# Two attention blocks on one core: when x's columns, q's pieces and small softmax steps are asked for in the v stage, and a new table of the main loop's order

## The chip, the cores and the metric

The kernel runs on one core of a Trainium2 chip. A core has five engines that each run their own instructions in program order: TensorE (PE in the profile, its weight loads PEld), VectorE (DVE), ScalarE (ACT), GpSimd (POOL) and SyncE (SP), which here starts nearly all transfers. The metric is the device time of one execution in microseconds; lower is better.

## The reference

Two independent attention blocks of 32 heads with 20 elements per head are computed on x of 2048 rows and 640 columns, and their outputs stand side by side. Block A looks at 8 earlier rows at a distance of 2 (a window); block B looks at all 2048 rows.

```python
# A
qkv = (x @ wqkv).reshape(B, S, 3, H, Dh)
idx = pos[:, None] - (jnp.arange(8) * 2)[None, :]
logits = einsum("bhsd,bhswd->bhsw", q, k[idx]) * Dh ** -0.5    # masked where idx < 0
a = einsum("bhsw,bhswd->bhsd", softmax(logits), v[idx]) @ wo
# B
scores = einsum("bhqd,bhkd->bhqk", q, k) * Dh ** -0.5
b = einsum("bhqk,bhkd->bhqd", softmax(scores), v) @ wo
return concatenate([a, b], axis=-1)
```

## The kernel before

All matrix products in fp32 are made of three products of a rounded high part and the rest (the list `PASSES`): high x high, high x rest, rest x high. A source that comes from memory lands in a staging tile `stg`; ScalarE copies it to the high part, and VectorE or GpSimd subtracts the high part from it for the rest. The stages, in order:

1. q and k of A, then q and k of B, for all rows. B's results go out to memory (`qb_d`, `kb_d`) and come back as stacks `bq` and `bk` of four heads (`b_pieces`). A stack of q has 16 pieces, four for each quarter of the rows.
2. **The v stage.** v of A and of B is computed in 15 blocks. Block 2c + half takes the column set c of x (0 to 3 are A's, 4 to 7 B's; a set is 512 rows of x, transposed, tiles `xn` and `xl`) and one half of the v weights (tiles `ww`). Each block has four ticks. In blocks 0 and 1 a tick is one group of 15 matmuls; from block 2 on a tick is 30 matmuls on half the array each, followed by four matmuls of one step of B's row maxima (`b_max`), which VectorE reduces (tile `mx`, two instructions a tick). `v_tick` closes a tick: it runs what is due then (`after(n, ...)` puts a step off by n ticks), asks for pieces of q, and lets GpSimd's work on A go on (`a_pace`, with an account of GpSimd's time, `gp.us`).
3. **The main loop**, 512 steps for B's 8 groups of heads. Each step needs four tiles of exponentials (tile `e`, ScalarE), four of maxima (VectorE), and four matmuls with v. The order of the tiles of 488 steps stands in a string, `ORDER`: S is two tiles for exponentials, M and N two tiles for maxima (reduced in one instruction or in two), Y one of each, V the step's matmuls with v, H a piece of A's output product, j a transpose for it; the digits are PSUM banks. The last 24 steps and B's last output follow from a plain loop.

GpSimd works through A's windows all this time: for each of 16 row tiles four units of scores (`akv` times `aq`, four adds, `al`) and four of values (`akv` times `al`, two adds), and the softmax between them; the reduce and the reciprocal of that softmax are VectorE's (`soft_jobs`). It also adds up B's parts (`braw`, `more`) and makes the rests of x's sets and of the v weights.

What the steps below touch: `x_load(c, w)` takes a set's tiles, asks for its three staging tiles at once and puts their copies and subtractions off by w ticks; it is called for set 1 after the first tick of block 0, and for set c + 2 at the end of block 2c + 1, each time with its copies one block later. `w_load(half, w)` does the same for B's v weights: half 0 at the end of block 4, nine ticks off; half 1 in the middle of block 7, four ticks off. Their subtractions, and those of sets 1 to 7, are GpSimd's. All transfers named here go through SP's queue in program order.

Of the kernel before, what the change touches and what calls it, by code (L numbers as in the profile page):

```python
# [75 lines left out]
def attention_pair(ctx, tc, xa, wqk_a, wv_a, wo_a, xb, wqk_b, wv_b, wo_b, oa, ob):  # L76
# [21 lines left out]
    soft_jobs, turn_jobs = [], []  # L98

# [478 lines left out]

    groups = 0
    gp.us = 0.0  # L580
    for m in range(0, 10, 2):
        nxt = []
        for n in range(4):
            for j in range(2):
# [355 lines left out]
    for block in range(15):  # L940
        c, half = divmod(block, 2)
        s0 = c % 4 * 4
        if block < 2:
            for s in range(s0, s0 + 4):
                v_group(c, half, s)
                v_tick(2.2, False)
                if (block, s) == (0, 0):
                    x_load(1, 5)
        else:
            ps4 = [bank() for _ in range(4)]  # L950
            for second in range(2):
                for u in range(2):
# [45 lines left out]
    def begin(i):  # L998
# [29 lines left out]
        "Y07M1S36Y54V0Y71S26M4Y03V7Y06M4S31Y72V0Y13M4S76VY71M2S64S05N17V6Y04M2S51VY70M4S13S26N07V1Y25S04N36VY07S25M3Y61"  # L1028
        "V0Y72M3S56VY75M1Y63S04V5Y06M1S74VY07S64M1Y35V0Y74S16Y23VM4S73Y61V2jY70M4S31VY07Y63M4S12S70Y63jV1jS72jM4Y03VM6"
        "S52Y40V3Y71jM5S24VY70M1S46S35Y07V4S31jM6Y52VY03S71Y65jM3S02Y57V1jM3S06Y72VjM3S05Y26V7Y01M3jS56VY05M1S36Y47V5"  # L1030
        "Y03M1S64VY07S64S31N25Y70V6jM4S32M0VS75M3S26jY01jV7jY25M3S61VY02S65M3jS71V0Y26M3S75VY71Y26H54Y30H54S71H54Y62H54"
        "Y73H54M1Y06V3Y74M1S05VY07M4S61Y23V7Y60S15N42VN06S51H43Y27H43Y05H43Y61Y27H43H43M5Y01V2Y73S04M5VY70M3Y15S62V0Y17"
        "M3S62VY71M5S24Y30V1Y27M5S43VY07H23N46S15H23Y70H23Y14H23Y56H23M0Y74V5S63M0Y72VS63Y74N01V2Y36S05Y74VM0S36Y54V7"
        "Y03M1S64VN06S53H42Y71H42Y05H42Y36Y71H42Y05H42Y36V7Y02M4S63VS06M2Y14V7M5S03Y21VM3S05Y62V1Y07M3S25VY07M5S42H31"
        "H31Y07H31Y24Y56H31Y07H31M4S26V0Y71S23M4VY71M2S46Y50V1Y74S26N35VY07S62M3H51H51Y07H51Y62M3H51Y07H51N62V0S17M3S56"
        "VM1S75Y43V6Y70S51M2VY70S15M2Y46V0S71jM2Y54VS71jY26S35N40V7jN64S21Y03VM5S42Y10V3jY47M5jS02VY70M1S64S53N07V6Y52"
        "S01M3VY70M1S53S46N07V5Y41M2S06VY70Y61S42Y35S07Y61N45V2Y01M3S75VY07S16M3S52N07V1S63M4Y02VY73S04M5Y21V7Y03M5S42V"
        "Y04M2S15Y76V0S15M2Y74VS15Y76Y23V0Y14S56N73VY71Y24H56Y03H56S71H56N42S03H56H56N74S01V2Y37M5S04VY70S13M5Y42V0Y17"
        "S63N54VY71M5S23Y40V1Y72S36N54VY07M5S23Y41V7Y02S63N54VN06S51H23Y74H23Y05H23Y16Y74H23Y05H23Y16V7Y02M4S63VY06S13"
        "M4Y27V6S01jM4S32jVjM0S75Y43V2jY01M6S35jVS01M3S57N62V0S13S45M6VM1S34Y76V5Y03S21N46VY70M2S14S65N07V1Y26S03M4VY07"  # L1040
        "M2S64S51N70V6Y52M3S71VY70M1Y53S46Y07V5Y64M1S03VY07M3S62S51Y07V6Y52S43N71VY70M4S32Y16V0Y73M4S21VY73M1S64H50H50"
# [145 lines left out]
```

## Time and profile before

| | us |
|---|---|
| median of three runs (1746.45 to 1746.90) | 1746.89 |
| the profiled execution | 1745.1 |
| its span from first to last instruction | 1742.9 |
| v stage with its blocks 2 to 14 and their tail, from 298.9 to 454.3 in the trace | 155.4 |
| main loop in the order of the table, 454.3 to 1626.0 | 1171.7 |

A row of the timeline is: start, length, engine, line, operation, output and input tiles, shape, count of instructions merged, and in brackets the idle time before it with what ended it. All instructions carry line 71, a helper that records them, so rows are told apart by the names of their tiles. A row of the windows gives each engine's busy time in a stretch, then the granted clock of TensorE, the busy share of the transfer engines, and GB/s.

### The profile page before, as it was taken

The page shows a single profiled execution, that of the slowest core. Times are in us where ns is not written, and L with a number is a line of the kernel's source. Part 1 is how long each engine was busy: PE and PEld are TensorE (multiplying, and loading weights), DVE is VectorE, ACT ScalarE, POOL GpSimd, SP SyncE. Part 2 cuts the span into 40 slices and gives each one's busy share as a digit, 9 for nine tenths or more (in the row PEclk, how much of TensorE's full clock was granted, in tenths as well). Part 3 has the DMA queues.
Part 4 walks back from the last instruction along what each step waited for, and adds up shares of the span by engine and source line. Part 5 has one row for each costly group of instructions (what it writes and reads, how often), then busy time and mean ns, then how long its engine had stood idle before and what let it go on. Part 6 is the DMA issues. An engine that isn't in the chain of part 4 may idle for free.

```text
span 1742.9 us, 34666 instructions
## 1 busy us (share of the span) xinstructions
PE 1726.1 (99%) x12711; PEld 1011.2 (58%) x12711; DVE 1349.3 (77%) x1818; ACT 1337.3 (77%) x2658; POOL 1271.9 (73%) x1125
## 2 busy tenths in 40 slices
PE   9999999999999999999999999999999999999999
PEld 8988888989635544444444443444444445444568
DVE  3113232888899999999999999999999999999300
ACT  4323223232599999999999999999999999999981
POOL 0000950999899999999999999999999953545242
PEclk9999999999999999999999999999999999999999
DMA  6447878657754263445435433543642532111123
GB/s 226 120 139 242 304 258 261 219 183 219 207 152 133 91 175 119 130 127 148 128 121 158 141 126 106 176 136 110 168 137 96 142 90 55 43 36 52 34 75 113
DMA packets 194435, 248.29 MB, mean 142 GB/s; under 512 B 89308, under 2 KB 114396, under 8 KB 193272
## 3 DMA queue, kind: packets, MB, share of 16 engines
q1 hardware_dynamic: 193688, 245.41, 46.6%
q8 instruction: 100, 1.64, 0.4%
q14 instruction: 71, 0.58, 0.1%
q10 hardware_dynamic: 576, 0.66, 0.1%
HBM read 181.08 MB, written 64.91 MB: 141 GB/s over the span
## 4 chain that ended last, share of the span: by engine, by line
PE 73%; POOL 17%; DMA 4%; issue 3%; DVE 2%; ACT 1%; SPq 1%; POOLq 0%; ACTq 0%; DVEq 0%
PE ps_st L71 73%; POOL akv L71 9%; POOL braw L71 4%; DVE mx L71 2%; POOL ao L71 1%; DMA stg<-xa 1%; SPq L71 1%; DMA mdr<-mtr 1%; DMA bq<-qb_d 1%; POOL ww L71 1%; POOL al L71 1%; ACT e L71 1%; DMA s_d<-braw 1%; POOL xn L71 0%; DMA s_d<-sm 0%
## 5 line engine op out<-in xcount | busy, mean ns | idle before, releaser
L71 DVE TENSOR_REDUCE mx<-ps_st 128x1 f32<-128x512 f32 (+1 forms) x1500 | 1227.5, 877 | 72.5 <-PE ps_st L71 61.4
L71 ACT ACTIVATE e<-ps_st 128x512 f32<-128x512 f32 x2048 | 1067.3, 630 | 32.5 <-PE ps_st L71 19.6
L71 PE MATMUL ps_st<-bk,bq 60*128 60x512 f32 x2048 | 555.1, 436 | 0.5 <-DVE mx L71 0.4
L71 PE MATMUL ps_st<-bq,bk 62*128 62x512 f32 x2048 | 548.7, 431 | 3.5 <-ACT e L71 1.8
L71 PE MATMUL ps_st<-e,vb 128*32 128x512 f32 x4096 | 543.1, 604 | 0.5
L71 PEld LDWEIGHTS ps_st<-bq,bk 62*128 62x128 f32 x2048 | 276.6, 184 | 401.6 <-ACT e L71 250.2
L71 POOL TENSOR_TENSOR braw<-braw,more 128x512 f32<-128x512 f32 x224 | 288.3, 1287 | 85.6 <-ACT more L71 85.1
L71 PEld LDWEIGHTS ps_st<-bk,bq 60*128 60x128 f32 x2048 | 257.9, 184 | 102.9 <-DVE mx L71 45.1
L71 POOL TENSOR_TENSOR akv<-akv,aq 128x1280 f32<-128x1280 f32 x64 | 188.4, 2944 | 166.4 <-DMA akv<-ka_d 166.3
L71 POOL TENSOR_TENSOR akv<-akv 128x640 f32<-128x640 f32 (+3 forms) x304 | 282.6, 930 | 14.7
L71 ACT COPY ro<-ps_st 128x320 f32<-128x320 f32 (+2 forms) x172 | 73.9, 465 | 185.9 <-PE ps_st L71 104.0
L71 PE MATMUL ps_st<-ww,xn 64*128 64x320 f32 (+1 forms) x1776 | 188.1, 311 | 6.5 <-POOL xn L71 2.4
L71 PEld LDWEIGHTS ps_st<-ww,xn 64*128 64x128 f32 (+1 forms) x1776 | 175.6, 187 | 22.6 <-ACT e L71 8.3
L71 PEld LDWEIGHTS ps_st<-e,vb 128*32 128x32 f32 x4096 | 82.2, 108 | 149.9 <-issue 77.1
L71 POOL TENSOR_TENSOR akv<-akv,al 128x1280 f32<-128x1280 f32 x64 | 151.6, 2368 | 0.1
L71 ACT COPY more<-ps_st 128x512 f32<-128x512 f32 x224 | 136.7, 610 | 4.0 <-POOL braw L71 2.0
L71 PE MATMUL ps_st<-xn,w 128*128 128x512 f32 x480 | 115.8, 390 | 0.0
L71 PEld LDWEIGHTS ps_st<-xn,w 128*128 128x128 f32 x480 | 90.1, 188 | 19.4
L71 POOL TENSOR_TENSOR xn<-stg,xn 128x512 fp32r<-128x512 f32 (+1 forms) x30 | 53.8, 1804 | 62.8 <-ACT xn L71 61.5
L71 PE MATMUL ps_st<-ww,aot 64*128 64x320 f32 x960 | 99.2, 308 | 0.0
L71 ACT CAST pr<-ps_st 128x512 fp32r<-128x512 f32 x40 | 23.5, 587 | 98.7 <-PE ps_st L71 93.0
L71 PEld LDWEIGHTS ps_st<-ww,aot 64*128 64x128 f32 x960 | 91.0, 186 | 4.6 <-DVE mx L71 0.5
(65 smaller groups left out, 1042.3 us busy)
## 6 DMA issues: line engine op xcount, KB each, us to landing
akv<-ka_d SPq DMA_DIRECT2D x128, 320.0 KB
akv<-va_d SPq DMA_DIRECT2D x128, 320.0 KB
kb_d<-pr SPq DMA_DIRECT2D x20, 512.0 KB
qb_d<-pr SPq DMA_DIRECT2D x20, 512.0 KB
bk<-kb_d SPq DMA_DIRECT2D x16, 640.0 KB
bq<-qb_d SPq DMA_DIRECT2D x64, 160.0 KB
stg<-xb SPq DMA_DIRECT2D x16, 512.0 KB
rb<-s_d SPq DMA_DIRECT2D x128, 64.0 KB
```

What stands on the lines that cost most here:

```text
L71: return self.tc.keep_in_program_order(op(*a, **k))
```

## The change

`x_load` is split. `x_raw(c)` takes only the three staging tiles and asks for them; `x_parts(c, raws)` later takes the set's tiles and issues copies and subtractions at once, with nothing put off. Set 1 is asked for in the last group but one of B's q and k, its parts come after the last tick of block 0, and their subtractions move from GpSimd to VectorE; set 2 is asked for at the same place. Set c + 2 is asked for after the first tick of block 2c + 1, and its parts come at that block's end. q's remaining 12 pieces are asked for one in a tick, and only in ticks with maxima (block 2 on), not two in each tick from block 0. VectorE's softmax steps in the v stage wait until they are due, where they had run at once. Half 0 of B's v weights is put off by eight ticks instead of nine. The string `ORDER` is new throughout; it has as many steps and as many pairs of tiles as before (Y, S, M and N: 698, 627, 444 and 127 before, 722, 615, 449 and 110 now, 1896 each time).

```diff
+    at_once = [True]
...
     def job(jobs, n, fn, *args):
         jobs.append((now[0] + n, fn, args))
-        if loop[0] is None:
+        if at_once[0]:
             run_jobs(jobs, 1)
...
+    def x_raw(c):
+        out = []
+        for a, b in PAIRS:
+            t = sb.tile([128, 1024], F32, tag="p", bufs=PB, name="stg")
+            raw = t[:, :(b - a) * 512].rearrange("p (k c) -> p k c", c=512)
+            sp.dma_start(raw, (xa, xb)[c // 4][a * 128:b * 128, c % 4 * 512:c % 4 * 512 + 512].rearrange("(k p) c -> p k c", p=128))
+            out.append((a, b, raw))
+        return out
...
                     elif g8 == 6:
                         for _ in range(4):
                             q_loads.pop(0)()
+                        xraw = x_raw(1)
...
     v_us = [40 * QK_US]
+    at_once[0] = False
...
-        for _ in range(min(2, len(q_loads))):
+        if maxima and q_loads:
             q_loads.pop(0)()
+        if soft_jobs and soft_jobs[0][0] <= now[0]:
+            run_jobs(soft_jobs, 1)
...
-    def x_load(c, w):
-        x, pieces = x_pieces((xa, xb)[c // 4], c % 4, gp)
-        XV.append((x, pieces))
-        wait[0] = w
-        for fn in pieces:
-            fn()
+    def x_parts(c, raws, second=gp):
+        t = columns(c % 4)
+        XV.append((t, None))
+        for a, b, raw in raws:
+            u, m = t[a // (KC - 1)], a % (KC - 1)
+            hi, lo = (u[:, x, m:m + b - a] for x in range(2))
+            act.copy(hi, raw)
+            second.tensor_tensor(lo, raw, hi.bitcast(F32), ALU.subtract)
...
-                if (block, s) == (0, 0):
-                    x_load(1, 5)
+                if (block, s) == (0, 3):
+                    x_parts(1, xraw, dve)
+                    xraw = x_raw(2)
...
                     v_tick(V_US)
+                    if half and c < 6 and not second and not u:
+                        xraw = x_raw(c + 2)
...
         if block == 4:
-            w_load(0, 9)
+            w_load(0, 8)
         if half:
             if c < 6:
-                x_load(c + 2, 4)
+                x_parts(c + 2, xraw)
...
     ORDER = (
-        "Y07M1S36Y54V0Y71S26M4Y03V7Y06M4S31Y72V0Y13M4S76VY71M2S64S05N17V6Y04M2S51VY70M4S13S26N07V1Y25S04N36VY07S25M3Y61"
+        "Y07S61M2Y45V0Y71S26M3Y05V7Y06M3S52Y71V0Y26M3S75VY71M5S24S03N17V2Y06S15Y34VM0S74Y56V3Y70S21N46VY70M4S12S63N07V1"
```

First place, SP at the change from B's q and k to the v stage, before (`pr` is a result of B's q, `ro` one of v's, `stg<-xa` a piece of set 1):

```order
L71 DMA bq_2015<-qb_d_70 20x1024
L71 DMA bq_2015<-qb_d_70 40x1024
L71 DMA qb_d_70<-pr_2153 128x2x512
L71 DMA va_d_69<-ro_2176 128x320
L71 DMA bq_2015<-qb_d_70 20x1024
L71 DMA bq_2015<-qb_d_70 40x1024
L71 DMA stg_2183<-xa 128x2x512
L71 DMA stg_2185<-xa 128x2x512
L71 DMA stg_2187<-xa 128x512
L71 DMA va_d_69<-ro_2204 128x320
```

The same place now:

```order
L71 DMA bq_2015<-qb_d_70 20x1024
L71 DMA bq_2015<-qb_d_70 40x1024
L71 DMA stg_2138<-xa 128x2x512
L71 DMA stg_2140<-xa 128x2x512
L71 DMA stg_2142<-xa 128x512
L71 DMA qb_d_70<-pr_2159 128x2x512
L71 DMA va_d_69<-ro_2182 128x320
L71 DMA va_d_69<-ro_2200 128x320
L71 DMA va_d_69<-ro_2224 128x320
L71 DMA va_d_69<-ro_2242 128x320
```

Set 1 moved ahead of a q store, a v store and two q pieces, and no q piece stands between the v stores any more.

Second place, GpSimd around half 1 of B's v weights, which block 9 needs, before (`ww_3323` is that half's rest, `xn_3415` and `xl_3416` that of set 5):

```order
L71 TENSOR_TENSOR akv_3099<-akv_3099,aq_2953 128x1280
L71 TENSOR_TENSOR ww_3323<-stg_3324,ww_3322 128x640
L71 TENSOR_TENSOR ww_3323<-stg_3326,ww_3322 128x640
L71 TENSOR_TENSOR ww_3323<-stg_3328,ww_3322 128x320
L71 TENSOR_TENSOR xn_3415<-stg_3417,xn_3415 128x1024
L71 TENSOR_TENSOR xn_3415<-stg_3419,xn_3415 128x1024
L71 TENSOR_TENSOR xl_3416<-stg_3421,xl_3416 128x512
L71 TENSOR_TENSOR akv_3099<-akv_3099 128x2x320
```

The same place now (`ww_3330` is the weights' rest, `xn_3431` and `xl_3432` set 5's):

```order
L71 TENSOR_TENSOR akv_3012<-akv_3012,aq_2872 128x1280
L71 TENSOR_TENSOR xn_3431<-stg_3286,xn_3431 128x1024
L71 TENSOR_TENSOR xn_3431<-stg_3288,xn_3431 128x1024
L71 TENSOR_TENSOR xl_3432<-stg_3290,xl_3432 128x512
L71 TENSOR_TENSOR ww_3330<-stg_3331,ww_3329 128x640
L71 TENSOR_TENSOR ww_3330<-stg_3333,ww_3329 128x640
L71 TENSOR_TENSOR ww_3330<-stg_3335,ww_3329 128x320
L71 TENSOR_TENSOR akv_3012<-akv_3012 128x2x320
```

Set 5's rest moved from behind the weights to ahead of them; the units of A ahead of both are the same in number and kind.

Third place, GpSimd early in the main loop, ahead of the first add of `braw`, before (`ww` is A's output weight there):

```order
L71 TENSOR_TENSOR akv_4541<-akv_4541 128x2x32
L71 TENSOR_TENSOR al_4544<-akv_4541 128x64
L71 TENSOR_TENSOR akv_4633<-akv_4633,aq_4244 128x1280
L71 CAST ww_4765<-stg_4845 128x640
L71 TENSOR_TENSOR ww_4766<-stg_4845,ww_4765 128x640
L71 CAST ww_4765<-stg_4869 128x320
L71 TENSOR_TENSOR ww_4766<-stg_4869,ww_4765 128x320
L71 TENSOR_TENSOR braw_4821<-braw_4821,more_4768 128x512
```

The same place now:

```order
L71 TENSOR_TENSOR akv_4551<-akv_4551 128x2x32
L71 TENSOR_TENSOR al_4420<-akv_4551 128x64
L71 CAST ww_4773<-stg_4853 128x640
L71 TENSOR_TENSOR ww_4774<-stg_4853,ww_4773 128x640
L71 CAST ww_4773<-stg_4879 128x320
L71 TENSOR_TENSOR ww_4774<-stg_4879,ww_4773 128x320
L71 TENSOR_TENSOR braw_4829<-braw_4829,more_4776 128x512
```

The multiplication `akv` by `aq` that stood among the weights' steps is no longer there; it came earlier, since one more unit of A's scores now stands in the v stage, where set 1's subtractions were.

## Rows read from the trace of the kernel before

**Rows 1.** windows: v stage from block 2, main loop (busy us, clock, DMA share, GB/s)

```profile
298.90:454.30 155.40, 148.95 (x1801) 139.23 (x1800) 125.20 (x115) 42.41 (x86) 143.07 (x111) 0.98 0.64 207
454.30:1626.00 1171.70, 1167.87 (x8671) 534.08 (x8670) 1137.02 (x1588) 1134.26 (x2274) 1022.09 (x904) 1.00 0.42 120
```

**Rows 2.** waits of ScalarE from 500 to 1640 (total, times, longest)

```profile
ACT e L71 <- PE ps_st L71: 19.2, 57, 0.9
```

**Rows 3.** timeline of VectorE: ticks 1, 29 and 52

```profile
308.87 2.36 DVE L71 TENSOR_REDUCE mx<-ps_st 128x2 f32<-128x1024 f32 x2 [20.08 <-PE ps_st L71]
...
387.30 2.36 DVE L71 TENSOR_REDUCE mx<-ps_st 128x2 f32<-128x1024 f32 x2 [0.92 <-PE ps_st L71]
...
449.53 2.36 DVE L71 TENSOR_REDUCE mx<-ps_st 128x2 f32<-128x1024 f32 x2 [0.33 <-PE ps_st L71]
```

**Rows 4.** timeline of TensorE (start, length, work, idle before and its releaser)

```profile
298.31 0.60 PE L71 MATMUL ps_st<-ww,xl 128*128 128x320 f32 x3
301.12 0.41 PE L71 MATMUL ps_st<-ww,xn 64*128 64x320 f32 x2 [2.21 <-ACT xn L71]
303.56 1.97 PE L71 MATMUL ps_st<-ww,xn 64*128 64x320 f32 x12 [2.02 <-POOL xn L71]
...
309.03 1.96 PE L71 MATMUL ps_st<-ww,xn 64*128 64x320 f32 x24
```

**Rows 5.** timeline of TensorE in block 8

```profile
372.90 1.14 PE L71 MATMUL ps_st<-ww,xn 64*128 64x320 f32 x12 [1.23 <-POOL ww L71]
```

**Rows 6.** windows: granted clock, after the busy times, in three stretches

```profile
372.00:374.00 2.00, 1.10 (x12) 0.88 (x12) 1.48 (x2) 0.00 (x0) 2.00 (x2) 1.00 0.08 19
302.00:303.00 1.00, 0.00 (x0) 0.00 (x0) 0.00 (x0) 1.00 (x4) 1.00 (x1) 0.63 0.77 274
...
308.00:309.00 1.00, 1.00 (x8) 0.83 (x6) 0.13 (x1) 0.00 (x0) 1.00 (x2) 0.50 1.07 400
```

**Rows 7.** the chain that ended last: one of its pieces (start, length, what)

```profile
290.92 6.25 DMA stg<-xa
```

**Rows 8.** timeline of ScalarE around the start of block 2

```profile
299.70 0.43 ACT L71 COPY ro<-ps_st 128x320 f32<-128x320 f32 x1 [4.90 <-DMA va_d<-ro]
300.02 1.99 ACT L71 CAST xn<-stg 128x1024 fp32r<-128x1024 f32 x2
```

**Rows 9.** timeline of SP's queue around the start of the v stage

```profile
279.71 1.51 SPq L71 DMA_DIRECT2D bq<-qb_d  x4
284.99 0.38 SPq L71 DMA_DIRECT2D qb_d<-pr  x1
...
289.62 1.26 SPq L71 DMA_DIRECT2D bq<-qb_d  x2
```

**Rows 10.** timeline of GpSimd, blocks 2 to 9

```profile
301.15 4.67 POOL L71 TENSOR_TENSOR xn<-stg,xn 128x1024 fp32r<-128x1024 f32 x2 [58.52 <-ACT xn L71]
...
307.00 0.46 POOL L71 TENSOR_TENSOR am<-al 128x128 f32<-128x128 f32 x1
...
340.23 4.76 POOL L71 TENSOR_TENSOR xn<-stg,xn 128x1024 fp32r<-128x1024 f32 x2 [2.95 <-ACT xn L71]
...
352.44 0.21 POOL L71 CAST mtr<-mtr 128x32 fp32r<-128x32 f32 x1 [1.20 <-DVE mtr L71]
...
382.57 3.93 POOL L71 TENSOR_TENSOR ww<-stg,ww 128x640 fp32r<-128x640 f32 x3
```

**Rows 11.** timeline of ScalarE early in the main loop

```profile
490.49 0.58 ACT L71 COPY more<-ps_st 128x512 f32<-128x512 f32 x1 [1.98 <-POOL braw L71]
```

**Rows 12.** timeline of GpSimd early in the main loop

```profile
482.65 2.94 POOL L71 TENSOR_TENSOR akv<-akv,aq 128x1280 f32<-128x1280 f32 x1
...
489.19 2.62 POOL L71 TENSOR_TENSOR braw<-braw,more 128x512 f32<-128x512 f32 x2
```

**Rows 13.** groups by shape: VectorE's reduces of the tiles (count, busy, mean ns)

```profile
L71 DVE TENSOR_REDUCE mx<-ps_st 128x2 f32<-128x1024 f32 x548 | 661.8, 1216 | 44.8 <-PE ps_st L71 42.7
L71 DVE TENSOR_REDUCE mx<-ps_st 128x1 f32<-128x512 f32 x952 | 615.0, 682 | 27.7 <-PE ps_st L71 18.7
```

More of the change, by code (lines that the diff above doesn't have):

```diff
@@ L1032, in attention_pair @@
[L1032 to L1041, printed above, removed]
@@ new lines, in attention_pair @@
+        "Y06H35M1Y74V0Y35M1S76VY73M4S62Y10V3Y76M4S21VY07M1S64Y53V7S60M1Y45VY06Y14H32Y75H32Y06H32Y14H32Y07H32M5Y41V0S72"
+        "M3Y56VY71S25M3Y60V7Y15M3S62VY06M1S53Y74V6S50N13Y27VY05Y41H23Y76H23Y05H23Y41H23Y07H23M4S61V0VY71M4S63H20H20Y17"
+        "H20Y36Y54H20Y17H20M5Y34V1S07M2Y65VY07S62M3Y51V0Y72S63M4VY71M2S64Y05V1Y74S26N30VN72S36H54Y01H54Y73H54Y62Y01H54"
+        "H54M6Y32V0Y15M6S43VY15M3S27Y06V5Y12S74N30VY76S41M2Y05V6Y74M2S10VY75H01Y24H01Y35Y76H01Y24H01Y35H01M6Y24V3S05M1"
+        "S76VjM4S70Y12V6jY75M3S02VY70S15M3Y26V0S71jM3Y52VY71S63M4S20jY71jV6Y52S43N01VN70S52Y43M6S51Y02V4Y35S76M0VY75M2"
@@ new lines, in attention_pair @@
+        "S60Y14V5Y67S03N21VY07S64M2Y15V7Y60M2S41VY06M4S13Y27V0Y16M4S32VY71M2S64Y05Y17V6Y02M3S51VY70M1S53S46N07V5Y41S02"
+        "Y63VM0S72Y34V6S75Y01N24VS75N31H02Y46H02S73H02Y15H02Y74H02N36S51V7Y02S63N45VY06S14M2Y57V6Y01S24N35VY70S14M2Y56"
+        "V0Y71M2S45VY71H65Y42Y03H65Y71H65Y42H65Y70H65M3Y21V7Y06S52M3VY06M1S53Y74V0jS35jM1S76jVjM3S57Y21V6jY05S43N71VY70"
+        "S52M3Y16V0Y75M3S21VY72M5S14Y30V2Y17M5S43VS70M3S15Y62V7S04M1Y35VY06M1S34S57N60V3Y24S15M6VY04M1S57S63N40V5Y67M1"
+        "S43VS07Y64S31N25V0Y72S64N53VY71M5S42S30N17V4Y35S62M0VY73M5S20H14H14Y73H14Y02Y56H14Y73H14S02N56V7Y01S35N64VY06"
@@ new lines, in attention_pair @@
+        "Y51S23Y47V6M0Y75S23VS70Y14N25V3S47Y06Y21VM6S05Y41V2Y30M6S15VY01Y35H76Y42H76M0S35H76Y24H76H76M0Y53Y24V7S06M1Y35"
+        "VY06S14M2Y57V0Y16M2S45VY71M4S63Y02S17V6M4S03Y21VM4Y70S13V2jY74S65M0VjY73S64M0S52jV3jM6S40Y15jVM6S02Y54M0S37Y26"
+        "V4Y57S30M1VY73M5S02S14N37V0Y16S52M3VY71M5S24S03N17V2Y06S15Y34VM0S74Y56V3Y70M1S46VY07S45M1Y63V7S04M1Y56VY04S53"
+        "Y21N67V0Y13M4S62VY71M2S64S05N71V6S02M3Y75VY02Y71H34Y56H34S02N71H34S56H34Y70H34M1Y56V0Y74M1S35VY73M4S62S10V3M6"
+        "S24Y51VM6S04Y12V5Y06M3S72VY07M1S36Y45V7Y03M1S64VS06M3S52Y17V0M3S56Y72VN13S46H52H52M0S74H52Y36H52H52M0S74Y36V5"
@@ new lines, in attention_pair @@
+        "Y70M1S64VY07S63M1Y45V7Y60M1S34VY06S53S42jN17jV6M0S53Y74VjM0S25Y43jV7jY60M1S35VY06M3S52S71Y60V5Y74M2S01VN74S06"
+        "Y32M0S75Y46V3Y72S01M4VY07M1S64Y35V7Y60S14M2VY06M4S13Y27V6Y01S53Y42VM0S72Y35V4Y07M1S56VY07S35M1S64N70V3Y21M6S45"
+        "VY04M1S57S63N40V5Y67S41M2VY07Y61S42H35N07H35S61H35Y40H35Y26H35M0Y74V6S53M0S72VM4S70Y13V2Y74M5S30VY71S34M5Y02V1"
+        "Y73M5S40VY72M3S05Y61V2S07N35Y46VY70Y13H45Y62H45Y70H45Y31H45H45M6S03Y21V4Y05Y76Y31VS07M5S32Y14V0jM5S73Y42VjM5"
+        "S71Y23V4jY05M6S13VjY05M1S37S64jY50V3M1S76Y04VM1S75Y64V0Y71S25M3VY71S26M3S50Y17V2M3S75Y06VM3S75Y61V0Y72M3S15V"
@@ new lines, in attention_pair @@
+        "Y71M5S42S30N17V4Y35S62M0VY73Y26S50M3S71Y26V5M3S07Y61VM3S70Y12V6Y75S04M2VY70M4S31S26N07V3Y24M0S56VY72H65S40N13"
+        "H65S72H65Y41H65Y70H65M1S34V0S75M1S63VM4S76Y12V3Y07M4S26VY70S12M4Y63V0Y71M4S26VY71M2S64Y50V1Y74M2S65VY07M5S42"
+        "H31H31Y07H31Y24Y56H31Y07H31M4Y26V0S71M2Y45VY71M2S46S50V7Y61M2S45VjM0S64Y32V5jY06S71N42VjY07M3S61Y25V0Y17M3S26V"
+        "S75M1S63Y04V7jY61S52M3jVM0S65S43Y27Y60S15N74V3M6Y02S41VY07M5S42V1Y07M3S56VY07M5S42Y31V7Y04M5S23VY04M2S15Y67V4"
+        "S01M2Y56VY70M2S15S64N70V1S23M5Y74VY02M5S73S41N02V7S63M4Y01VY62S03M4S17N62V0S13M4Y76VY13Y72H45Y60H45S31H45Y72"
@@ new lines, in attention_pair @@
+        "Y25M3S06VY07M5S24S31N70V2Y36S75Y14VM6S05Y43V1Y02M6S53VY02M4S73S61N20V7Y63M4S21VY06M2S14S75N60V1Y72S36M4VY07M2"
+        "S64Y51V0Y74M2S56VY71M4S63Y20Y17V6Y52M3S01VY70M1S53S46N07V5Y41M2S06VY70Y61M2S45Y07V6Y51M2S04VY70M4S13S26N07V1"
+        "Y25M3S06VY07M5S24S31N70V2S36M4Y71VS03M4S76Y12V0Y73M4S62VY71S63Y24Y50S17N64V3M5S02Y41VM5Y70S12V4Y35M6S01VY05M2"
+        "S71S64N50V7Y61S25M3VY06M1S53S74N60V5Y71S62M3VY07M1S63S45N70V6Y14M2S75VY70M4S13S26N07V1Y25M3S06VY07M5S24S31Y07"
+        "V2Y36M4S71VM6S03S54N12V0Y73M5S14VY71M2S46Y05Y17V4Y03M5S21VY70M2S16S45N07V1Y26S03M4VY07M2S64S51N70V6Y52M3S71V"
@@ L1088, in attention_pair @@
+        "Y70M1S53S46N07V5Y41M2S06VY70Y61M2S45Y07V6Y51M2S04VM0S75M2S46S70N15V4Y37S62M0VM6S53M0S24")
     owed = []
```

77 lines of the change are left out of this document (28 added, 49 removed).

## The prediction

> **What bounds the kernel now.** I read the windows by stage first. In the main loop VectorE is busy 1137.0 of 1171.7 us and ScalarE 1134.3; TensorE shows 1167.9, but its weight loads only 534.1 [rows 1]. So ScalarE and VectorE, both near 97%, set the pace there, and what the loop can still give are their waits: ScalarE's for tiles from TensorE come to 19.2 us in 57 waits [rows 2]. In the v stage ScalarE is nearly free (42.4 of 155.4) and GpSimd is the fullest engine after TensorE (143.1), so I then read TensorE's waits in that stage, and for each the engine that ended it.
>
> A tick of that stage takes (449.53 - 387.30) / 23 = 2.706 us [rows 3]. Block 1's last matmul ends at 298.31 + 0.60 = 298.9 [rows 4]. The first tick's maxima should be reduced a tick later, at 301.6; the row says 308.87: 7.3 us lost. The next 28 ticks should take 75.8 and take 387.30 - 308.87 = 78.4: 2.7 lost, at blocks 8 and 9, where TensorE waits for GpSimd's part of the weights; block 8's longest wait is 1.23 [rows 5]. So 10.0 us can be had in this stage.
>
> The 7.3 us consist of 4.6 idle (2.21 and 2.02 in the rows, and a short third wait, seen as the rest of the sum) and 2.7 of slow matmuls: 12 took 1.97 from 303.56, while 24 took 1.96 from 309.03 [rows 4]. Between them the granted clock is 0.50, TensorE's 1.2 GHz level, after 0.63 from 302 to 303 [rows 6]; before it fell, the engine had done two matmuls since 298.9. The cause: set 1 is asked for at 290.92 and lands 6.25 later [rows 7], and ScalarE gets to its copies only at 300.02, since a copy of v ahead of them had waited 4.90 for an earlier store that stood in SP's queue among q's pieces [rows 8].
>
> **The first wait goes: -7.3.** Set 1's three transfers now stand right behind the first four pieces of q. What stood next there before started at 284.99, and a transfer two places later at 289.62 [rows 9]. I give the first piece the former time, the third the latter; with 6.25 us each, they land from 291.2 to 295.9. ScalarE's copies take 2.0 and some 0.6 for the small one and need not wait for the second half of v's copies. VectorE's subtractions are hidden: it has nothing to do until 301.6. Even at GpSimd's price for a set, 307.00 - 301.15 = 5.9 [rows 10], begun at 291.2 and with 1.3 left for the last piece, they end near 297.3, ahead of 298.9. Bounds: 0 (the transfers land as before) and -7.3; I take -7.3, with 1.6 us to spare. With no q piece between v's stores until block 2, the stores are not held; each later q piece is needed a quarter of the maxima (16 ticks) or more after its place, so a late one costs nothing, and if one held the queue it would be by about a 6 us transfer against a set now asked for three ticks (8 us) ahead of its parts.
>
> **GpSimd becomes the limit at block 9: +7.0, against the 2.7 lost at blocks 8 and 9 before.** GpSimd has no work from A until v's first rows are stored, so its long stretch begins with the first x set given to it: set 1 at 301.15 before, now set 2. ScalarE copies block 1's last group (0.43 after 298.9, ends 299.4) and starts on set 2; before, GpSimd started 1.1 after ScalarE [rows 8, 10]. That gives 300.5: only 0.6 earlier, though TensorE is now 7.3 earlier. From there to the first piece of weights' half 1 GpSimd took, before, 382.57 + 1.57 - 301.15 = 83.0 us (1.57 is 640 of the 1600 columns of the 3.93), of which 2.95 and 1.20 were waits [rows 10]: 78.8 of work. In its new order set 1 (5.9) is gone, but set 5 of the same size stands ahead of the weights instead of behind them; A's units between are the same. So the piece is ready at 300.5 + 78.8 = 379.3.
>
> Without stalls TensorE would begin block 9 at 301.6 + 28 ticks - one tick = 374.7, and stops after two pairs of matmuls, at 375.0. It stands idle for 4.3 us. Half 0 of the weights, for block 8, comes 14.7 us of GpSimd work earlier (half 0, a unit's adds and product, set 5), near 364.6, and block 8 wants the last of it about 365: no stall, 1 us to spare. After the idle stretch I take the slow clock at the price of the first wait, 2.7. Sum: 4.3 + 2.7 = 7.0, and block 9's first reduce near 384.4 instead of 387.30. Bounds: 0 (GpSimd is 5 us faster than I count) and +11 (its two waits, 4.15, come again). I take 7.0, since the rows used are those of the same instructions.
>
> What the clock does here decides 1.9 us. Rows: a wait of 1.23 in block 8 left it at 1.00, the stretch from 298.9, with two matmuls in it, took it to 0.50 [rows 5, 6]. The Trainium skill, "TensorE: Matmul & The Clock Gate", section "What's actually happening", says the slow clock is the default state and that activity lifts it, so that one long gap costs more than the same time in short ones; that speaks against this change, which trades several gaps for one. By that rule the sum stands as above; if the clock stayed up, the second and third piece of the weights would be waited for instead, as before (384.1 to 387.30 is 3.2 us), the reduce would come at 382.5, and the time would be 1.9 us lower.
>
> **Start of the main loop: -1.5.** ScalarE waits 1.98 there for GpSimd's first add of `braw` [rows 11], which starts at 489.19, after a product of 2.94 that now stands earlier [rows 12]. GpSimd's load in the v stage changes by one unit of A's scores (2.96 for the product, 6.8 in all) less set 1 (5.9): +0.9, and TensorE comes some 3 us earlier; GpSimd starts 0.6 earlier and may save up to 4.2 of waits. Against TensorE it stands between 0.9 earlier and 3.3 later, with 2.9 freed ahead of the add: the wait lies between 0 and 2.4. I take 0.5 left.
>
> **Small softmax steps put off: 0.** A reciprocal between two ticks fits into VectorE's slack of about 0.3 in a tick (2.36 busy of 2.706 [rows 3]); GpSimd needs the results ticks later, by then they have run.
>
> **The new table: 0.** The pairs are 1896 before and after. VectorE does 5 more double reduces and 10 fewer single ones: 5 x 1.216 - 10 x 0.682 = -0.7 us [rows 13], not on one path. What the table can change are waits like ScalarE's 19.2 us; from none of them left to twice as many is -19.2 to +19.2. Nothing in the rows says which, so I take 0.
>
> **Sum.** -7.3 + (7.0 - 2.7) - 1.5 = -4.5. Span 1742.9 - 4.5 = 1738.4; with the 2.2 around it (1745.1 - 1742.9) 1740.6 for an execution like the profiled one. The median of the runs is 1.8 above that execution, so 1742.4.
>
> **Rivals.** *The clock stays up* at block 9: 1740.5. For: short waits leave it at 1.00. Against: the one stretch of similar length did not. *GpSimd is not late*: all of 10.0 and 2.0 is won, 1734.9. For: nothing but its 4.2 us of waits, which are counted as gone already. Against: the same instructions in the same number. *Given back*: block 9 as forecast, but GpSimd's waits come again in part, or the main loop's first wait stays, or the table costs 1 to 3 us: 1744 to 1748, about 1745.5. *Slower, the table*: the order of the 1896 pairs lets ScalarE wait for TensorE more often. For: 57 waits of 0.34 on average show how easily a pair comes late, and the whole order is new. Against: same pairs, same banks. It decides from 7.8 us more on (the 4.5 won, and 3.5 to be told from no change), 23 further waits of 0.34; at half as many again, 9.6 us, the time is 1752.
>
> **How the numbers follow.** Forecast 0.45 (its own range 1739.5 to 1745.5), clock up 0.15, GpSimd not late 0.08, given back 0.19, table slower 0.13. What a measurement of this kernel can tell from no change is 0.2%, 3.5 us: under 1743.4 is faster, over 1750.4 slower. Two thirds of the forecast's chance (0.30), 0.15 and 0.08 lie under it: faster 0.53; same 0.15 + 0.19 = 0.34; slower 0.13. The range leaves out most of the case GpSimd not late below and of the table above: 1736 to 1749.5.
>
> **What would show it.** Right: the first reduce of the maxima a tick after block 1's end; TensorE idle for 4 to 5 us near the 29th tick, released by GpSimd's `ww`, with a clock of 0.50 behind it; GpSimd without a gap from about 300.5 to there; tick 52 near 446.6. Wrong: no wait on `ww` at block 9 (then GpSimd started earlier than I think), ScalarE still waiting for `stg` or for v stores ahead of block 2, or, with the v stage as told, a main loop that is not 1170 us within some 3.

## The result, and the profile after

| | before | after |
|---|---|---|
| median of the runs | 1746.89 | 1754.53 (1752.62 to 1755.19) |
| profiled execution, its span | 1745.1, 1742.9 | 1755.19, 1753.4 |
| forecast | | 1742.4 |

The changed kernel is slower: 1.0045 of the time before, interval 1.003 to 1.006, some 7.6 us. The v stage went much as the forecast says. First VectorE's timeline of the changed kernel, the rows that answer to [rows 3] (tick 1, the tick behind block 9's wait and the next, tick 52):

```profile
302.44 2.36 DVE L71 TENSOR_REDUCE mx<-ps_st 128x2 f32<-128x1024 f32 x2 [3.09 <-PE ps_st L71]
...
385.49 2.36 DVE L71 TENSOR_REDUCE mx<-ps_st 128x2 f32<-128x1024 f32 x2 [7.65 <-PE ps_st L71]
388.76 2.36 DVE L71 TENSOR_REDUCE mx<-ps_st 128x2 f32<-128x1024 f32 x2 [0.91 <-PE ps_st L71]
...
448.27 2.36 DVE L71 TENSOR_REDUCE mx<-ps_st 128x2 f32<-128x1024 f32 x2 [0.33 <-PE ps_st L71]
```

Tick 1 is 6.4 us earlier than before (308.87), tick 52 only 1.3 (449.53). Between them TensorE stands still once, at block 9, as its timeline shows (to compare with [rows 4, 5]), and runs slowly behind that, as the windows show (granted clock behind the busy times, as in [rows 6]):

```profile
299.31 2.42 PE L71 MATMUL ps_st<-ww,xn 64*128 64x320 f32 x24 [0.61 <-ACT ro L71]
...
381.19 3.04 PE L71 MATMUL ps_st<-ww,xn 64*128 64x320 f32 x20 [5.22 <-POOL ww L71]
```

```profile
384.00:385.00 1.00, 1.00 (x10) 1.00 (x10) 0.00 (x0) 0.00 (x0) 0.98 (x1) 0.50 0.74 291
...
387.00:388.00 1.00, 1.00 (x17) 1.00 (x16) 0.85 (x1) 0.00 (x0) 0.92 (x3) 1.00 0.00 0
```

GpSimd's timeline ([rows 10] before) and ScalarE's ([rows 8]) tell why block 9 waited a little longer than forecast. GpSimd begins at 302.33 where 300.5 was forecast. About 1.1 us of that is ScalarE's: it had four copies of v left at 298.84, behind set 1's casts and a wait of 0.82 for a store, and was done with them at 300.47 instead of 299.4. The other 0.74 is its wait for set 2, which had only just landed. From 302.33 GpSimd needs 379.60 + 1.55 - 302.33 = 78.8 us to the first piece of the weights (1.55 is 640 of the 1600 columns of the 3.87).

```profile
302.33 4.77 POOL L71 TENSOR_TENSOR xn<-stg,xn 128x1024 fp32r<-128x1024 f32 x2 [59.66 <-PE ps_st L71]
...
379.60 3.87 POOL L71 TENSOR_TENSOR ww<-stg,ww 128x640 fp32r<-128x640 f32 x3
```

```profile
295.14 1.05 ACT L71 CAST xn<-stg 128x1024 fp32r<-128x1024 f32 x1 [4.78 <-DMA stg<-xa]
...
298.84 1.63 ACT L71 COPY ro<-ps_st 128x320 f32<-128x320 f32 x4 [0.82 <-DMA va_d<-ro]
301.21 1.05 ACT L71 CAST xn<-stg 128x1024 fp32r<-128x1024 f32 x1 [0.74 <-DMA stg<-xa]
```

The loss is in the main loop, and it is one event. The windows below count ScalarE's tiles of `e` done since 440 (length, ScalarE's busy time with the count, clock, transfers), before:

```profile
440.00:500.00 60.00, 36.07 (x70) 1.00 0.63 181
440.00:600.00 160.00, 120.54 (x231) 1.00 0.52 150
440.00:1291.00 851.00, 726.00 (x1391) 1.00 0.48 140
440.00:1320.00 880.00, 751.73 (x1440) 1.00 0.48 138
440.00:1640.00 1200.00, 1028.55 (x1972) 1.00 0.42 120
```

and after:

```profile
440.00:500.00 60.00, 39.54 (x77) 1.00 0.60 172
440.00:600.00 160.00, 121.70 (x233) 1.00 0.51 148
440.00:1291.00 851.00, 728.44 (x1396) 1.00 0.48 138
440.00:1320.00 880.00, 744.29 (x1426) 0.99 0.48 138
440.00:1640.00 1200.00, 1022.06 (x1958) 1.00 0.42 119
```

In the three windows up to 1291 the changed kernel leads by 2 to 7 tiles; at 1320 it is 14 behind, and at 1640 still 14. In 29 us it lost 19 tiles; before, a tile takes (1291 - 600) / (1391 - 231) = 0.596 us, so 11.3 us. What happened there is in the waits of VectorE from 500 to 1640 (total, times, longest), which before had no wait for `al`, and in ScalarE's, of which there were 57 before, none over 0.9 [rows 2]:

```profile
DVE mx L71 <- PE ps_st L71: 18.5, 57, 1.5
DVE am L71 <- POOL al L71: 9.5, 1, 9.5
```

```profile
ACT e L71 <- PE ps_st L71: 28.2, 54, 9.9
```

VectorE's timeline of the changed kernel at that place; `am<-al` is the maximum of A's softmax for the sixteenth and last row tile, the reciprocal is the fifteenth's:

```profile
1291.41 0.34 DVE L71 RECIPROCAL am<-am 128x32 f32<-128x32 f32 x1
...
1301.22 0.59 DVE L71 TENSOR_REDUCE am<-al 128x32 f32<-128x256 f32 x1 [9.46 <-POOL al L71]
```

In the kernel before, the same two, and then GpSimd's addition that finishes `al`, of before and of after:

```profile
1301.02 0.34 DVE L71 RECIPROCAL am<-am 128x32 f32<-128x32 f32 x1
...
1310.10 0.62 DVE L71 TENSOR_REDUCE am<-al 128x32 f32<-128x256 f32 x1
```

```profile
1308.19 0.32 POOL L71 TENSOR_TENSOR al<-akv 128x64 f32<-128x64 f32 x1
```

```profile
1300.86 0.32 POOL L71 TENSOR_TENSOR al<-akv 128x64 f32<-128x64 f32 x1
```

Before, the maximum came 1310.10 - 1308.51 = 1.6 us after GpSimd was done: a margin that no view of waits shows. After, it stands right behind the reciprocal. VectorE's order, first before, then now (`mx4` are the reduces of the tiles, and the dots stand for five more reduces and a transpose):

```
L71 RECIPROCAL am_14159<-am_14159 128x32
L71 TENSOR_REDUCE mx4_14534<-ps_st_66 128x2
L71 TENSOR_REDUCE mx4_14534<-ps_st_66 128x1 x3
...
L71 TENSOR_REDUCE mx4_15015<-ps_st_66 128x1 x3
L71 TENSOR_REDUCE am_14948<-al_14447 128x32
```

```
L71 RECIPROCAL am_14028<-am_14028 128x32
L71 TENSOR_REDUCE am_14878<-al_14437 128x32
```

The thirteen instructions between the two are gone. The rule that puts it there is in `a_attention`: when the values of a row tile begin (`c == 4`), `run_jobs(soft_jobs, 1)` runs the oldest waiting softmax step, whichever tile it belongs to. Following the program by its rules: before, that was the reciprocal, due a step of the loop later. In the changed kernel's arrangement of GpSimd's steps the reciprocal had become due in that same step and had run; the oldest was the maximum, asked for a moment earlier, and it ran five steps ahead of its time. VectorE then stood at this instruction, TensorE had no free bank and waited for VectorE, and ScalarE had no tiles (TensorE's row and ScalarE's). Behind the wait the clock was low (the windows of all engines: granted clock 0.50 for 5 us):

```profile
1303.06 0.79 PE L71 MATMUL ps_st<-bk,bq 60*128 60x512 f32 x2 [9.48 <-DVE mx L71]
```

```profile
1304.31 1.57 ACT L71 ACTIVATE e<-ps_st 128x512 f32<-128x512 f32 x3 [9.89 <-PE ps_st L71]
```

```profile
1291.00:1301.00 10.00, 2.58 (x20) 0.93 (x16) 0.75 (x2) 3.42 (x7) 9.76 (x11) 0.85 0.34 105
1301.00:1306.00 5.00, 2.94 (x14) 1.03 (x14) 4.36 (x7) 1.57 (x3) 4.92 (x4) 0.50 0.01 3
```

### The profile page after: what moved, and what is told of

It is laid out like the page before. It is cut to its first block, busy times and chain, and to the rows that moved or that the text cites. A ratio compares the mean times of both kernels' runs of the same rounds, so it can differ in the third digit from the quotient of the medians.

```text
span 1753.4 us, 34676 instructions
## 1 busy us (share of the span) xinstructions
PE 1727.3 (99%) x12711; PEld 1006.0 (57%) x12711; DVE 1350.3 (77%) x1816; ACT 1339.1 (76%) x2658; POOL 1266.3 (72%) x1122
## 3 DMA queue, kind: packets, MB, share of 16 engines
q8 instruction: 100, 1.64, 0.4%
## 4 chain that ended last, share of the span: by engine, by line
PE 82%; POOL 9%; DVE 3%; DMA 3%; ACT 2%; issue 1%; SPq 1%; ACTq 0%; POOLq 0%
PE ps_st L71 82%; POOL akv L71 4%; DVE mx L71 3%; POOL braw L71 2%; ACT e L71 1%; DMA bq<-qb_d 1%; SPq L71 1%; POOL ao L71 1%; POOL aot L71 1%; DMA va_d<-ro 0%; DMA akv<-ka_d 0%; DMA stg<-xa 0%; POOL al L71 0%; ACT more L71 0%; DMA tr_d<-turn 0%
## 5 line engine op out<-in xcount | busy, mean ns | idle before, releaser
L71 PE MATMUL ps_st<-bk,bq 60*128 60x512 f32 x2048 | 561.0, 437 | 10.8 <-DVE mx L71 9.7
L71 DVE TENSOR_TENSOR pr<-ps_st,pr 128x512 fp32r<-128x512 f32 x40 | 27.6, 691 | 86.4 <-ACT pr L71 86.4
```

The lines of the kernel that those rows point to most:

```text
L71: return self.tc.keep_in_program_order(op(*a, **k))
```

## The experiments

The kernel before was measured again beside each group of runs, and its medians lie from 1745.77 to 1746.89. Medians of kernels from different groups can differ by as much for no reason of the kernels; each ratio is to the kernel before of its own group.

**The one wait taken away.** The changed kernel, with the last tile's maximum asked for a unit of A later, as for the other tiles:

```diff
         yield
-        if t < NT - 1:
-            yield
+        yield
         m = sb.tile([128, 4, H], F32, tag="am", bufs=2, name="am")
```

> The changed kernel with one edit: the maximum of the last row tile's softmax (VectorE's reduce am<-al of 128x256) is asked for one unit of A later, so that it stands some 13 instructions later on VectorE. Theory A (one wait): the changed kernel's whole loss is VectorE's 9.46 us at 1291.8 for GpSimd's al, with the 1.8 us of slow TensorE clock behind it. Until 1291 the changed kernel was 5 tiles of e ahead of the one before, at 1320 it was 14 behind: 19 tiles of 0.587 = 11.2 us. Then the time is 1754.5 - 11.2 = 1743.3, between 1741.5 and 1745, faster than before by 0.2%, and VectorE's waits for al in the main loop are under 1 us. Rival B (the table is slow as a whole): the wait comes back at another place, on GpSimd or on ScalarE, and the time stays over 1751.

Measured: 1744.77, ratio to before 0.9994 (0.9985 to 1.0003). VectorE has no wait for `al`; ScalarE's waits for tiles are 17.6 us in 52. The place of this one instruction accounts for 1754.53 - 1744.77 = 9.8 us by the medians (8.9 by the two ratios), and theory A holds, 1.5 us above its forecast. The 0.2% below the kernel before that it also gave is not shown: the interval includes 1.

**The wait put into the kernel before.** The same maximum run as soon as it is asked for:

```diff
         job(soft_jobs, 5, lambda: dve.tensor_reduce(m[:, 0], ...
+        if t == NT - 1:
+            run_jobs(soft_jobs, 9)
         yield
```

> The kernel before with one edit: the last row tile's maximum is run on VectorE as soon as it is asked for, right behind the reciprocal of the tile before it, which is some 9 us earlier than it stood (1310.10, when GpSimd's al had ended at 1308.51). Theory A (this place alone costs the loss): VectorE waits about 7.5 us for al, and with the slow clock after it the time grows by 8 to 10 us, to 1755 to 1757. Rival B: the banks and tiles in flight cover the wait, ScalarE goes on, and the time stays within 2 us of 1746.9.

Measured: 1755.58, ratio 1.0055 (1.0041 to 1.0068). VectorE's timeline of this kernel has the wait, and the time lies where the changed kernel's does: the place of this one instruction is enough for the loss.

```profile
1311.46 0.59 DVE L71 TENSOR_REDUCE am<-al 128x32 f32<-128x256 f32 x1 [7.87 <-POOL al L71]
```

**The table undone.** The changed kernel with the old string:

```diff
     ORDER = (
-        "Y07S61M2Y45V0Y71S26M3Y05V7Y06M3S52Y71V0Y26M3S75VY71M5S24S03N17V2Y06S15Y34VM0S74Y56V3Y70S21N46VY70M4S12S63N07V1"
+        "Y07M1S36Y54V0Y71S26M4Y03V7Y06M4S31Y72V0Y13M4S76VY71M2S64S05N17V6Y04M2S51VY70M4S13S26N07V1Y25S04N36VY07S25M3Y61"
```

> The changed kernel with the string ORDER of the kernel before; the v stage is the changed one. Theory A (the one wait comes from where the new order puts the step, and the v stage is faster): the last maximum stands again a few steps later on VectorE, no wait of 9 us, time 1746.9 - 1.3 (tick 52 was at 448.27 against 449.53) - 1.5 (wait at the start of the main loop) = 1744.1, between 1742 and 1746.5. Rival B (GpSimd comes late out of the changed v stage, whatever the table): the wait of VectorE for al is there again with 5 us or more, and the time is 1750 or more. Rival C (the table alone is worth the loss as a sum of small waits): no long wait, but e1 stays slow and this is 1744.

Measured: 1749.02, ratio 1.0012 (1.0004 to 1.0021). There is no wait for `al`: the maximum ran at 1303.81, GpSimd was done at 1298.2. So the changed v stage does not bring the wait by itself: rival B falls. Nor does the new table by itself, as far as the program tells. With the new string in the kernel before (which was not run) the same rules take the reciprocal there, two steps before it is due, and fifteen instructions of VectorE stand between it and the maximum. The place comes from the two edits together: each shifts GpSimd's steps a little, and only both make the reciprocal due in the step in which the row tile's values begin. The time is 5 us over theory A's, and rival C is half right: ScalarE's waits for tiles (the same view as above) are more than before and more than with the new table:

```profile
ACT e L71 <- PE ps_st L71: 22.4, 69, 0.9
```

Against the kernel of the first experiment (same v stage, new table, no long wait) the old table costs 1749.02 - 1744.77 = 4.3 us, about what ScalarE's waits differ by (22.4 and 17.6). With the new table these waits hardly depend on what the v stage does: 17.3 to 18.4 us in the ten kernels of this section that have it. In the changed kernel the table therefore did two things: it saved 4.3 in many small waits, and, together with the v stage, cost 9.8 in one.

**Block 9's wait.** The first experiment's kernel, with half 1 of the weights put off by two ticks, so that GpSimd makes it ahead of set 5:

```diff
                 if block == 7 and not second and u:
-                    w_load(1, 4)
+                    w_load(1, 2)
```

> As the kernel with the later maximum, and besides half 1 of B's v weights is put off by two ticks instead of four, so that GpSimd makes its rest ahead of set 5's. Theory A: the first piece is ready near 373.7 + 1.6 = 375.3 instead of 381.2, TensorE reaches block 9 at 375.5, so of the 7.9 us lost there (5.2 idle, 2.7 slow clock) some 1 stays: 6.9 less, time 1743.3 - 6.9 = 1736.4, between 1735 and 1739. Rival B: GpSimd as a whole is the limit, and sets 6 and 7 or the first adds of the main loop are then waited for instead: 3 us or more given back, 1740 to 1743.

Measured: 1740.37, ratio 0.9968 (0.9955 to 0.998), the fastest of the kernels, faster than before by 0.3% and than the changed one by 14.2 us. The main loop's first single reduce comes at 445.18 instead of 453.31: 8.1 us won in the stage, the whole of the 5.2 idle and the slow clock. 4.4 of them arrive at the end. The time is in rival B's range, but the place is one that it did not name, the seam to the main loop: 1.64 + 0.56 us of waits for ScalarE's copies of v (`ve`), and a mean granted clock of 0.91 from 440 to 460. TensorE's timeline there, and SP's:

```profile
446.99 0.49 PE L71 MATMUL ps_st<-bq,bk 62*128 62x512 f32 x1 [1.64 <-ACT ve L71]
448.04 0.73 PE L71 MATMUL ps_st<-bk,bq 60*128 60x512 f32 x3 [0.56 <-ACT ve L71]
```

```profile
431.68 0.44 SPq L71 DMA_DIRECT2D vb<-vb_d  x1
439.63 1.73 SPq L71 DMA_DIRECT2D mdr<-mtr  x4
441.41 0.90 SPq L71 DMA_DIRECT2D akv<-ka_d  x2
442.48 0.57 SPq L71 DMA_DIRECT2D bq<-mdr  x2
443.09 1.79 SPq L71 DMA_DIRECT2D vb_d<-ve  x4
```

SP stands still from 432.1 to 439.6, for GpSimd's rest of `mtr`, with v's stores behind it, for which ScalarE and then TensorE wait. Four kernels try to get this back, each an edit on the weights-first kernel.

*v's stores by ScalarE's queue* (`after(1, act.dma_start, vb_d[...` for `sp`):

> As the kernel with the weights first (1740.4), and besides the stores of B's v (vb_d<-ve) are started by ScalarE's queue instead of SP's. In that kernel ScalarE's copy of ve at 446.5 waited 6.10 us for such a store, which stood on SP behind mdr<-mtr; that one waited for GpSimd's cast of mtr (SP idle from 432.1 to 439.6). TensorE lost 1.64 + 0.56 there and had a mean clock of 0.91 from 440 to 460 (1.8 us). Theory A: these 4.0 us at the end of the v stage go, some of it is lost again before 500: 1736.5 to 1738.5, forecast 1737.3. Rival B: the stage's end is not on the path, because GpSimd's work for the output weights holds the main loop's start: 1739.5 to 1741.

Measured: 1748.17, ratio 1.0008 (0.9999 to 1.0017): 7.8 slower, neither theory. The last stores, started from 445.2 on, held ScalarE until 456.5 and TensorE for one wait of 8.86 us; `bk<-kb_d` went out on SP's queue at the same time. That it held the stores is likely but not shown. The trace is of a run of 1745.69, 2.5 below the median.

*Set 2 asked for a tick sooner* (`x_raw(2)` after the third tick of block 0), on top of that:

> As the kernel with the weights first and ScalarE's stores, and besides set 2 is asked for one tick sooner (after the third tick of block 0). In the changed kernel set 2 landed late: ScalarE waited 0.74 for it at 301.21 and GpSimd began at 302.33, where 300.5 was forecast. Theory A: GpSimd begins 1.5 to 2 us sooner and every later step of it too, since it is full from there on; the time falls by 0 to 1 us, as no wait of TensorE for GpSimd is left in the v stage but short ones. Rival B: GpSimd is the limit of the whole stage and the main loop's start, and the time falls by the whole 1.8. Rival C: set 2's transfers hold SP's queue ahead of v's stores and the time grows by 1 to 3.

Measured: 1750.88, ratio 1.0026 (1.0017 to 1.0035), 2.7 more than without: rival C. The three transfers now stand ahead of v's fourth store, ScalarE's copy of v ahead of set 2's waited 3.21 us for it, and GpSimd began at 304.35, not sooner than 301.35 but 3.0 later.

*mtr by VectorE in the v stage* (`e = dve if loop[0] is None else gp`), stores on SP again:

> As the kernel with the weights first (1740.4), ve stored by SP again, but in the v stage the cast and the rest of mtr (128x32, 0.21 and 0.25 us on GpSimd) are made by VectorE right behind its transpose, so that SP's mdr<-mtr need not wait for GpSimd. Theory A: there VectorE's transpose came 7 us ahead of GpSimd's cast, SP stood idle from 432.1 to 439.6, and the stores of ve behind it came late, which cost TensorE 1.64 + 0.56 idle and some 1.8 of slow clock. With the queue free the stores go in time: 1740.4 - 4 + what the loop's start takes back (up to 1.5) = 1737 to 1738. VectorE's 0.46 more in three ticks fit the slack of 0.3 in a tick and the next. Rival B: SP then waits at the next transfer that GpSimd frees a buffer for (akv<-ka_d), as late as before: 1740, within 1.

Measured: 1742.56, ratio 0.9978 (0.9968 to 0.9987): 2.2 over the weights-first kernel, though the two intervals overlap, and neither theory. The seam's gain came: TensorE does not wait for `ve` there any more. But VectorE could not do the two small steps in 0.46 us while GpSimd was at work, and TensorE waited for VectorE at each of the three transposes: 0.78 and 0.63 us near 349, 0.43 near 393, 3.17 and 0.33 near 440. The main loop's first single reduce comes at 454.39, 9.2 later than in the weights-first kernel. VectorE's timeline at the third transpose, and GpSimd's at the same time:

```profile
434.59 1.34 DVE L71 CAST mtr<-mtr 128x32 fp32r<-128x32 f32 x1
435.97 2.84 DVE L71 TENSOR_TENSOR mtr<-mtr 128x32 fp32r<-128x32 f32 x1
```

```profile
434.32 1.57 POOL L71 TENSOR_TENSOR ao<-ao,akv 128x640 f32<-128x640 f32 x1
435.86 2.91 POOL L71 TENSOR_TENSOR akv<-akv,aq 128x1280 f32<-128x1280 f32 x1
```

*The transfers of `mtr` put off by three ticks*:

```diff
-        after(t + 2, store)
-        after(t + 3, load)
+        d = 3 if loop[0] is None else 0
+        after(t + 2 + d, store)
+        after(t + 3 + d, load)
```

> As the kernel with the weights first (1740.4), but in the v stage the transfers of a quarter's maxima (mdr<-mtr and bq<-mdr) are put off by three ticks, GpSimd's part of mtr staying where it is. There the third of them held SP's queue from 432.1 to 439.6, and the four stores of ve behind it went at 443.09. Theory A: SP now waits only for the buffer of akv<-ka_d, which GpSimd frees at 436.2; the stores go by 439, TensorE's 1.64 + 0.56 at 447 and the slow clock of 440 to 460 (1.8) go, and up to 1.5 of it is lost at the loop's start, where GpSimd's output weights stand: 1740.4 - 4.0 + 1 = 1737.4, between 1736.5 and 1738.5. Rival B: the transfers moved hold the next set's or q's tiles somewhere else, or the loop's start takes all of it: 1740 to 1742.

Measured: 1742.90, ratio 0.9982 (0.9973 to 0.9991). The stores went at 437.82 and TensorE's waits at the seam are gone, as theory A says, but rival B has the time, 2.5 over the weights-first kernel (these two intervals overlap as well). By 469.78 ScalarE is 3.9 us ahead of that kernel (the same copy to `more` starts there at 473.72), which is theory A's 4.0; then it waited 2.32 us for TensorE at 480.1 and 3.20 for GpSimd's `braw` at 484.9, and at 488.26 it is 1.8 behind (486.51). GpSimd's add of `braw` starts at 483.60 here and at 481.14 there, behind A's output weights, for whose transfers GpSimd waited 1.29 and 0.44 us.

**q's pieces as before.** The first experiment's kernel with the old two pieces a tick:

```diff
-        if maxima and q_loads:
+        for _ in range(min(2, len(q_loads))):
             q_loads.pop(0)()
```

> As the kernel with the later maximum (1744.8), but q's pieces are asked for two in each tick from block 0 on, as in the kernel before: 10 of them stand between v's first stores and set 2's transfers. Theory A: set 1 still lands in time, but the stores of v are held, ScalarE's copies of v wait again (4.90 us before), and set 2 comes later to GpSimd, so that block 9 waits longer by as much: 2 to 5 us more, 1747 to 1750. Rival B: only set 1's place counted, the pieces are harmless: within 1 us of 1744.8.

Measured: 1750.98, ratio 1.0022 (1.0013 to 1.0031), 6.2 more: theory A, 1 us over its range. Each of ScalarE's four copies of block 1's v waits 0.86 to 0.99 for a store, tick 1 moves to 305.68, GpSimd begins at 309.09, 6.8 later than in the changed kernel, and the main loop 6.5 later (459.77 for 453.31). Block 9 does not wait longer, as theory A has it: 5.46 us for 5.30, since TensorE is late by itself.

**The softmax steps at once, as before** (`at_once[0] = False` only at the main loop):

> As the kernel with the later maximum (1744.8), but VectorE's softmax steps in the v stage run at once, as in the kernel before. The reduce am<-al that ran at 337.12 then stands five ticks of 2.706 earlier, at 323.6, and GpSimd's al ended at 323.92; the one at 428.82 comes to 415.3, al ended at 412.65. Theory A: a wait of about 0.3, which the slack of a tick takes: 1744.8, within 1. Rival B: GpSimd is later against VectorE than before, VectorE waits for al in the middle of a tick, TensorE stands behind it and its clock falls: 3 us or more, over 1748.

Measured: 1743.91, ratio 0.9986 (0.9977 to 0.9995): theory A. VectorE's 0.99 us for `al` at 324.31 is taken back at block 9, where TensorE now waits 4.23 instead of 5.30. With block 9's wait gone this cover is gone too:

> As the kernel with the weights first (1740.4), but VectorE's softmax steps in the v stage run at once, as in the kernel before. With the later maximum alone VectorE's wait for al at 324.3 was 0.99 us, and TensorE's wait at block 9 was shorter by as much (4.23 for 5.30): it was hidden there. Theory A: with block 9's wait gone that cover is gone too, and the 0.7 us of it over a tick's slack show: 1741, between 1740 and 1742. Rival B: the deferral costs more elsewhere (GpSimd waits for VectorE's results): 1739 to 1740.

Measured: 1741.73, ratio 0.9972 (0.9961 to 0.9983), 1.4 over the weights-first kernel: theory A's side, though its interval and that of the weights-first kernel overlap. With `mtr` by VectorE as well:

> The two edits together: mtr by VectorE in the v stage, and the softmax steps at once there. Theory A of each: 1737 to 1738 for the first and 0.7 more for the second: 1738.3. If SP still waits for GpSimd's buffers: 1741.

Measured: 1742.64, ratio 0.9984 (0.9975 to 0.9993): no sum of gains. The time is nearer the second case; its trace (of a run of 1747.27, one of the slowest of eleven) shows TensorE waiting for VectorE at the transposes again, 2.05 and 0.63 us near 351 and 3.60 and 0.63 near 402.

## Why the prediction was wrong

- **The first wait goes: -7.3.** Right, 6.4 measured, but without the 1.6 us to spare. The first piece of set 1 reached ScalarE at 295.14, not 291.2 (asked for at 285.15, it took some 10 us and not 6.25), and VectorE's part of it ended at 298.67 + 0.69 = 299.36, not 297.3; TensorE did not wait for it. ScalarE's copies of v behind set 1's casts came late: one waited 0.82 for a store, and TensorE began block 2 after 0.61 idle. ScalarE's waits for `stg` and for a v store ahead of block 2 are a sign of being wrong that the forecast itself names.
- **GpSimd becomes the limit at block 9: +7.0.** Right in mechanism and nearly in size. The 78.8 us of work came out as 78.8; its start did not (302.33 for 300.5): the forecast gave ScalarE one copy of v between block 1 and set 2 where there were four (1.1 us), and did not ask when set 2's own transfer lands (0.74). So 5.22 idle for 4.3; the clock behind it was 0.50, as the forecast took it, not the rival's 1.00. The rule of the Trainium skill cited there ("TensorE: Matmul & The Clock Gate", "What's actually happening") agrees with this place: the one wait of 5.22 was followed by the low clock, where the 1.23 in block 8 before was not. Tick 52 came at 448.27 for 446.6.
- **Start of the main loop: -1.5.** Wrong in what lasts. The wait of [rows 11] is gone from its place (by 500 the lead is 7 tiles, 4.2 us, of which 1.3 are the v stage's), but ScalarE waits for `braw` at later adds instead, 1.15 us at 514.21 and 0.62 at 529.42, which are nearly the 1.98 of before; by 600 the lead is 2 tiles.
- **Small softmax steps put off: 0.** Right within the error: 1743.91 with them at once, 1744.77 without, and overlapping intervals; with the weights first it is 1741.73 and 1740.37, the other way.
- **The new table: 0.** This step failed. It priced only ScalarE's waits for TensorE, between none and twice as many, as many small ones; those improved (4.3 us against the old table). What decided was a wait that the main loop before did not have: VectorE's for GpSimd's `al`, 9.46 us, worth 9.8 in the time. And it priced the table apart from the v stage, while the two together moved the maximum. The rival of a slower table had the right part of the change and the wrong mechanism; its 23 further small waits did not come, there were 54 for 57.
- Without that one wait the kernel measures 1744.77, 2.4 above the 1742.4; beside 1746.16 for the kernel before that is 1.4 less, where 4.5 were forecast, and not told from no change.
- By its own terms the rival of the table decides from 4.5 + 3.5 = 8.0 us on, not 7.8; nothing turns on it.

ScalarE's two waits for `braw` in the changed kernel, for the third step above:

```profile
514.21 0.58 ACT L71 COPY more<-ps_st 128x512 f32<-128x512 f32 x1 [1.15 <-POOL braw L71]
...
529.42 0.59 ACT L71 COPY more<-ps_st 128x512 f32<-128x512 f32 x1 [0.62 <-POOL braw L71]
```

The evidence for the failed step was there. The forecast counted the waits of before, and this place had none: it had a margin of 1.6 us, where for the tile ahead the maximum had come 14.1 us after GpSimd's `al` was done (1250.46 and 1236.00 + 0.32). And the new order of VectorE shows the instruction thirteen places earlier.

What stays open: that the loop's start takes back what the v stage wins is shown as a change of waits (`ve`, then `braw`, which stands behind A's output weights on GpSimd), and no run takes that work away; the new table with the old v stage was followed in the program only; and why the old table has more small waits behind the changed v stage than behind the old one (69 for 57) was not tried.

## What to carry to other kernels

When an order is rewritten, list the instructions that wait for the engine that runs late, and compare for each the margin in the trace before (its start minus the releaser's end) with how far the order moves it; a place with no wait and a small margin, 1.6 us here, is one that a reordering can turn into a long wait. Do this with all edits in place, not with one at a time: here neither the table nor the v stage moved the instruction alone. A rule that runs "the oldest waiting step" whoever it belongs to can turn one step of shift into an instruction five steps early. And where one engine is full for hundreds of microseconds, as GpSimd is here, a wait taken from another engine can come back at the next thing that the full one delivers, so such a gain is worth what arrives at the end (4.4 of 8.1 here), not what the stage shows.

## What the hardware did that was not expected

In the kernel with `mtr` on VectorE its cast and subtraction of 128x32 took 1.34 and 2.84 us at 434.59 and 435.97 (the rows above), and 1.09 and 0.68 at 345.63 and 346.76. Only once, at 391.07, did the subtraction take 0.19. The long ones ended within 0.06 us of the end of the GpSimd instruction that ran beside them: 435.93 and 438.81, where GpSimd's two ended at 434.32 + 1.57 = 435.89 and 435.86 + 2.91 = 438.77; 346.72 and 347.44, where they ended at 346.69 and 347.38. So does the cast of 0.33 at 390.71: it ended at 391.04, GpSimd's instruction at 391.00. The subtraction of 0.19 began at 391.07, 0.01 us before GpSimd's next (391.08). So each looks held until GpSimd's instruction was over, unless VectorE began first.

The Trainium skill, "SBUF — State Buffer", section "Who interferes with whom", says that VectorE and GpSimd share a pair of ports that one instruction takes as a whole, that a VectorE instruction with two inputs in SBUF stands against a GpSimd instruction that reads SBUF, that a cast can take the pair too, and that the order of issue decides which of the two waits. The trace agrees, to 0.06 us. Such a wait shows as a longer instruction and not as idle time before it, so no view of waits has it under VectorE; it shows as TensorE's wait for VectorE.
